# Transposing the gated product of tiles 2 to 14 by 32x32 squares on VectorE and a copy through DRAM instead of on TensorE

## The chip, the cores and the metric

The kernel runs on one core of a Trainium2 chip. The metric is the device time of one execution in microseconds. Engines are named as in the profile: PE (TensorE, with PEld for its weight loads), DVE (VectorE), ACT (ScalarE), POOL (GpSimd), SP (SyncE, whose queue issues nearly all transfers).

## What is computed

Three steps in a row, on 2304 tokens (4 sequences of 576) with 512 features:

```python
scores = scale * (q @ k.T); scores = where(0 <= i - j < 64, scores, -1e9)      # 8 heads of 64
x = softmax(scores) @ v                                                        # [2304, 512]
x = ((x @ w_a) * (x @ w_b)) @ w_out                                            # d_ff = 1536
logits = x @ phi                                                               # 32 slots, 4 for each of 8 experts
slot_input = softmax(logits, over tokens).T @ x
slot_out[e] = relu(slot_input[e] @ w1[e]) @ w2[e]                              # 512 -> 1024 -> 512
out = softmax(logits, over slots) @ slot_out
```

The weights moe_w_a, moe_w_b and moe_w_out arrive as doubles and are turned into float32 on the chip.

## The kernel before

Tokens are worked on in 18 tiles of 128. The gated product g = (x @ w_a) * (x @ w_b) of a tile is [128 tokens, 1536], made in three blocks of 512 columns, each in two halves: twelve matmuls into psa, which ACT copies to SBUF, and twelve into psb, which DVE multiplies with that copy into g (line 459). (The third block's halves are 24 matmuls of half the width.) w_out is never applied to the tokens: w_out @ phi is computed once (wphi, by project_phi), so the logits are g @ wphi, and the slots gather sums of g, which pass through w_out at the end.

The logits contract over the 1536 columns of g, so g is needed with its columns on the partitions. r_t does that for one block: four PE transposes of 128x128 (by the helper at line 142) into a PSUM tile, and an ACT copy into gT. r_l then runs twelve matmuls per tile (the profile counts two passes of each, so 24), wphi as weights and gT as the moving operand, into four groups of 32 partitions (lps). r_k, r_d and r_u follow: running maxima and sums over the tokens, a softmax over the slots, and g weighted by it into the sums acc.

PE's order is written out by hand. Its unit is a slot: the events entered for that slot with `at`, then one half block of the product. A tile has six slots in the steady state. With done[t, 2] for the slot of a tile's last half block, the logits r_l stand at slot R[t], and R[t] is done[t, 2] + 3 or, where that is later, four slots after the tile before. In a slot, the attention of a tile two further on (att_s, att_n, att_pt, att_pv, att_q, att_k) stands ahead of the r_ events. The start (up to slot 24) is a list of its own, STARTUP, in which the blocks of tiles 0 and 1 are transposed. The other engines' orders, SP's queue included, are laid out by the compiler's scheduler, from readiness and the order of the program; each engine runs its own in order.

SP issues the loads of q, k and v (lda is the 128 rows of v that begin 64 rows ahead of the tile, ldb the tile's own), each into a single buffer, at slots tied to the attention that frees it. At slot lastA = 93, when the attention of the last tile is done, open_ex gives its memory and other buffers to the experts' weights, and fetch starts to load: first w_out's float32 copy (wo_dram), then w1 and w2, into slots in a fixed sequence: two "as1", two "gT1" (buffers of gT), three "e" of the pool ex1, then seven "y", "z", "g" and so on. The pool ex1 holds the raw w_out and w_b pieces during the start, and nothing between then and these loads.

Of the kernel before, what the change touches and what calls it, by code (L numbers as in the profile page):

```python
# [11 lines left out]
F32 = mybir.dt.float32  # L12
# [51 lines left out]
HUGE = 3.0e38  # L64
# high words of the doubles 2**-127 and (just under) 2**128, read as float32
DBL_LO = float(np.array([896 << 20], np.int32).view(np.float32)[0])
# [4 lines left out]
def swa_glu_softmoe_kernel(  # L71
# [50 lines left out]

# [1 line left out]
    ident = const.tile([P, P], F32, name="ident")  # L124
# [10 lines left out]
    def turn(tag):  # L135
        """The tag's two halves in turn; the first alone once the second holds what the end needs."""
        t = turns[tag]
        t[0] = (t[0] + 1) % t[1]
        return f"{tag}{t[0]}"
# [40 lines left out]

# [1 line left out]
    att_stack = ExitStack()  # L182
# [38 lines left out]
    def att_z():  # L221
        """Zeros in the place of each pair's other head."""
        nc.gpsimd.memset(qTs, 0.0)

    # the first tiles' q as it is, two tiles in turn; the others' with zeros beside each head's part
    def att_q(t):
# [80 lines left out]
    def att_n(t, b):  # L307
        """The rows' sums divide."""
        st = sts[t]
        h = slice(4 * b, 4 * b + 4)  # L310
        rs = small.tile([P, 4, 1], F32, tag="rs", name="rs")
        r2 = rs.rearrange("p u o -> p (u o)")
        nc.vector.tensor_scalar(out=r2, in0=st["sm"][:, h], scalar1=EPS, scalar2=None, op0=ALU.add)
        yield
        nc.vector.reciprocal(out=r2, in_=r2)
        yield
        pr = st["pr"][b]
        eng = nc.gpsimd if t <= NFIRST else nc.vector
        eng.tensor_tensor(out=pr, in0=pr, in1=rs.to_broadcast([P, 4, P]), op=ALU.mult)  # L319
# [35 lines left out]

# [1 line left out]
    whi, wlo = {}, {}  # L357
# [4 lines left out]
    def decode(t, st):  # L362
        """Raw doubles st [P, n, 2] to float32 t [P, n]; out of float32's range: to 0 or its largest."""
        hi, lo = st[:, :, 1], st[:, :, 0]
        i = t.bitcast(I32)
        nc.scalar.activation(out=t, in_=hi.bitcast(F32), func=ACTF.Abs)
        yield
        nc.vector.tensor_scalar(out=t, in0=t, scalar1=DBL_LO, scalar2=DBL_HI, op0=ALU.max, op1=ALU.min)  # L368
        yield
        nc.vector.tensor_scalar(  # L370
            out=i, in0=i, scalar1=3, scalar2=0x3FFFFFF8, op0=ALU.logical_shift_left, op1=ALU.bitwise_and
        )
        yield
        nc.vector.scalar_tensor_tensor(  # L374
            out=i, in0=hi, scalar=-(1 << 30), in1=i, op0=ALU.bitwise_and, op1=ALU.bitwise_or
        )
        yield
        nc.vector.scalar_tensor_tensor(  # L378
            out=t.bitcast(U32), in0=lo.bitcast(U32), scalar=29, in1=t.bitcast(U32),
            op0=ALU.logical_shift_right, op1=ALU.bitwise_or,  # L380
        )
        yield
# [5 lines left out]

    # chunk j of a block: rows 128j.., all 512 columns; of the last block rows 256c.., columns 256h.., j = 2h + c
    def stage_w(nm, fg, j):  # L390
# [43 lines left out]
    def glu(t, fg, nm, halves=None):  # L434
        """Half of a block of the product: x @ w_a, or x @ w_b and the product of both."""
        if t not in gts:
            gts[t] = gp.tile([P, DFF], F32, tag="g", name="g")
        xhi, xlo = xts[t]
        if fg < NFG - 1:
            parts = [(0, slice(0, 512))]  # L440
        else:
            parts = [(h, slice(256 * h, 256 * h + 256)) for h in (halves or range(2))]
        ps = ps_ab.tile([P, 512], F32, tag=nm, name=f"ps{nm}")
        for h, cols in parts:
            n = 0
            for kk in range(KD):
                wh, wl = w_part(whi, nm, fg, kk, h), w_part(wlo, nm, fg, kk, h)
                for l, r in ((xhi, wh), (xhi, wl), (xlo, wh)):
                    nc.tensor.matmul(ps[:, cols], lhsT=l[:, kk], rhs=r, start=(n == 0), stop=(n == 3 * KD - 1))  # L449
                    n += 1  # L450
                yield
        cols = slice(parts[0][1].start, parts[-1][1].stop)
        if nm == "a":
            asb = p2.tile([P, 512], F32, tag=turn("as"), name="asb")
            nc.scalar.copy(out=asb[:, cols], in_=ps[:, cols])  # L455
            pas[t, fg] = asb
        else:
            gcols = slice(512 * fg + cols.start, 512 * fg + cols.stop)
            nc.vector.tensor_tensor(out=gts[t][:, gcols], in0=ps[:, cols], in1=pas.pop((t, fg))[:, cols], op=ALU.mult)  # L459

# [1 line left out]
    stats = {}  # L462
    rst = {}

    def r_t(t, fg):
# [6 lines left out]
        rst[t, fg] = gT  # L472

    def bank(t, shape, nm):
        """A PSUM tile of the token tile t's routing: the last ones run beside each other."""
        if t < NTILE - 2:
            return ps_m.tile(shape, F32, tag="m", name=nm)
        return ps_s.tile(shape, F32, tag=f"s{t % 2}", name=nm)

    def r_l(t, fgs=range(NFG)):  # L480
        lps = bank(t, [P, P], "lps")
        for n, fg in enumerate(fgs):
            gT = rst.pop((t, fg))
            for i in range(4):
                nc.tensor.matmul(  # L485
                    lps[32 * i:32 * i + 32], lhsT=wphi[:, 4 * fg + i], rhs=gT[:, i],
                    start=(n == 0), stop=(n == len(fgs) - 1),
                )
# [8 lines left out]
    def r_k(t):  # L497
        """Running maxima and sums of the slots over the tokens."""
        l4 = rst[t, "l4"]
# [32 lines left out]
    def r_c(t, lk=None):  # L532
        """Softmax of a token over the slots."""
        l4 = rst.pop((t, "l4"))
# [39 lines left out]
    def project_phi(c):  # L574
        """Rows 128c.. of w_out: to float32, kept in DRAM, and times phi."""
        st = stage(ex1, "e", moe_w_out[P * c:P * c + P, :])
# [23 lines left out]

# [1 line left out]
    cts = {}  # L602
    c4s = {}

    def both(t0, tag):
        """Both parts of the tokens' softmaxes, twice."""
        n = min(4, NTILE - NLAST - t0) if t0 < NTILE - NLAST else NLAST
# [11 lines left out]
    def turn_c(t0, bank):  # L619
        """The slots to the partitions."""  # L620
        c, n = c4s.pop(t0)
        cp = bank[0].tile([P, 4, P], F32, tag=bank[1], name="cp")
        for i in range(n):
            transpose(cp[:, i], c[:, i].bitcast(F32).rearrange("p a s -> p (a s)"))
        cps[t0] = (cp, n)
# [9 lines left out]

# [1 line left out]
    exw = {}  # L637
    pool_bufs = {**wbufs, "y": N_EX2, "z": N_EX3}
    slot_halves = {"g": 3, "as1": 1, "gT1": 1, "z": 1}
    # halves of 2 KB in the order of their use  # L640
    order = [("o", c) for c in range(DFF // P)]
# [12 lines left out]
    def source(key):  # L654
        """Rows of an expert's weights that a half of a slot takes, and those that may follow in one transfer."""
        if key[0] == "o":
# [9 lines left out]
    def fetch(n=0):  # L666
        """Fills the next n slots, or all whose contents have been used."""
        while nxt[0] < len(order):
# [40 lines left out]

# [1 line left out]
    units = [(0, 0), (1, 0), (0, 1), (1, 1), (2, 0), (2, 1), (3, 0), (3, 1)] + [(t, 2) for t in range(NFIRST)]  # L711
# [17 lines left out]
    for t in range(NTILE - 1, NFIRST - 1, -1):  # L729
        sA[t] = min(first[t] - 6, sA.get(t + 1, NSLOT) - 3)  # L730
    R = {}
    for t in range(NTILE - NLAST):
        R[t] = max(done[t, NFG - 1] + 3, R[t - 1] + 4 if t else 24)
    for t in range(NFIRST, NTILE):
# [15 lines left out]
    for t in range(NTILE):  # L750
        if t < NTILE - NLAST:
            r = R[t]
            at(max(done[t, 0] + 2, r - 5), r_t, t, 0)
            at(max(done[t, 1] + 2, r - 3), r_t, t, 1)
            at(max(done[t, 2] + 1, r - 2), r_t, t, 2)
            at(r, r_l, t)
# [8 lines left out]
    for n, f, t, *x in (  # L765
# [5 lines left out]
        at(NSLOT + n, f, t, *x)  # L771
    lastA = sA[NTILE - 1] + 5
    lastfg = {fg: done[NTILE - 1, fg] + 1 for fg in range(NFG)}
# [23 lines left out]
    def run(f, *a):  # L797
        """All of a work's pieces, each for one engine."""
        pieces = f(*a)
# [33 lines left out]

# [1 line left out]
    _, sden = stats[NTILE - 1]  # L835
# [94 lines left out]
    def slots_pick(n, c):  # L930
        """Of each expert's rows those of its own slots."""
        if c == 0:
# [82 lines left out]
```

## Time and profile before

| | |
|---|---|
| median of 3 runs | 579.15 us (578.6 to 579.62) |
| span of the profiled execution | 577.4 us |
| PE busy | 540.5 us, 94% |
| DVE busy | 297.6 us, 52% |
| ACT busy | 229.8 us, 40% |
| moved by DMA | 83.00 MB |

The profile is of one execution. Its span runs from the first instruction of the program to the last; its own whole time isn't listed, so the median of the runs stands beside the span, 1.75 us above it. Times inside the profile are counted from the start of the span. In the chain of waits each piece is the work that the next one waited for, or the one before it on the same engine.

### The profile page before, as it was taken

The numbers are of one execution on the slowest core, as the hardware profiler recorded it, in microseconds if no ns is written. First come the engines' busy times: TensorE is split into PE (matmuls) and PEld (weight loads), VectorE is DVE, ScalarE is ACT, GpSimd is POOL, SyncE is SP. The second block draws the span as 40 slices with busy tenths as digits, with TensorE's granted clock in tenths as the row PEclk, the third lists the DMA queues.
The fourth block names the chain that finished last, engine by engine and source line by source line (L and its number), as shares of the span: only waits on it lengthen the run. The fifth ranks groups of instructions, "written<-read, shape, count | busy, mean of one in ns | idle before, by whom it ended". The sixth has DMA issues, their size and how long they took to land.

```text
span 577.4 us, 11537 instructions
## 1 busy us (share of the span) xinstructions
PE 540.5 (94%) x4531; PEld 429.9 (74%) x4531; DVE 297.6 (52%) x861; ACT 229.8 (40%) x675; POOL 76.5 (13%) x110
## 2 busy tenths in 40 slices
PE   4588899999999999999999999999999999989993
PEld 3476667889887879787888888888888767953442
DVE  3999999974444444353634443454555311142222
ACT  5767664544524343443523333433454211133013
POOL 4555465331000000000000000000000000020000
PEclk9789899999999999999999999999999999999997
DMA  9975747495030302020212203022212499889997
GB/s 267 266 224 182 242 137 212 145 257 183 0 75 1 75 18 58 18 57 19 56 27 48 56 19 74 17 59 56 56 38 74 152 351 339 317 289 346 341 357 245
DMA packets 110822, 83.00 MB, mean 144 GB/s; under 512 B 77616, under 2 KB 98608, under 8 KB 110768
## 3 DMA queue, kind: packets, MB, share of 16 engines
q1 hardware_dynamic: 109808, 79.12, 46.2%
q0 software_dynamic: 960, 3.15, 1.4%
q8 instruction: 36, 0.59, 0.4%
q14 instruction: 18, 0.15, 0.1%
HBM read 74.38 MB, written 7.86 MB: 142 GB/s over the span
## 4 chain that ended last, share of the span: by engine, by line
PE 77%; DVE 13%; DMA 4%; issue 2%; ACT 1%; SPq 1%; POOL 0%; POOLq 0%; ACTq 0%
PE psb L449 24%; PE psa L449 23%; PE tg L142 5%; PE s L283 4%; PE xps L342 3%; PE lps L485 3%; PE tp L142 2%; PE ups L560 2%; PE h L883 2%; DVE w L374 2%; DVE w L378 2%; PE ops L917 2%; DMA st<-in_moe_w_a_dram 2%; DVE w L368 1%; PE tq L142 1%
## 5 line engine op out<-in xcount | busy, mean ns | idle before, releaser
L449 PE MATMUL psa<-wha,x 128*128 128x512 f32 (+1 forms) x576 | 160.4, 347 | 2.1 <-DVE x L352 1.2
L449 PE MATMUL psb<-whb,x 128*128 128x512 f32 (+1 forms) x576 | 161.3, 348 | 1.1 <-DVE g L459 1.1
L449 PEld LDWEIGHTS psa<-wha,x 128*128 128x128 f32 x576 | 101.4, 189 | 18.3 <-DVE x L352 2.0
L449 PEld LDWEIGHTS psb<-whb,x 128*128 128x128 f32 x576 | 101.3, 190 | 14.7 <-issue 2.4
L449 PE MATMUL psa<-wla,x 128*128 128x512 f32 (+1 forms) x288 | 97.3, 338 | 1.2 <-POOL wla L424 1.2
L449 PE MATMUL psb<-wlb,x 128*128 128x512 f32 (+1 forms) x288 | 97.2, 337 | 0.0
L459 DVE TENSOR_TENSOR g<-psb,asb 128x512 f32<-128x512 f32 (+1 forms) x57 | 37.7, 661 | 89.2 <-PE psb L449 75.0
L455 ACT COPY asb<-psa 128x512 f32<-128x512 f32 (+1 forms) x57 | 32.1, 563 | 103.8 <-PE psa L449 103.4
L301 ACT ACTIVATE pr<-pr,nmx 128x128 f32<-128x128 f32 x144 | 55.9, 391 | 36.7 <-DVE nmx L294 36.7
L449 PEld LDWEIGHTS psa<-wla,x 128*128 128x128 f32 x288 | 54.7, 190 | 6.9 <-POOL wla L424 2.1
L449 PEld LDWEIGHTS psb<-wlb,x 128*128 128x128 f32 x288 | 54.8, 190 | 4.6 <-POOL wlb L424 0.2
L471 ACT COPY gT<-tg 128x512 f32<-128x512 f32 x54 | 31.4, 584 | 37.1 <-PE tg L142 37.0
L252 POOL COPY kTs<-kTs 128x256 f32<-128x256 f32 x17 | 8.2, 480 | 270.8 <-DVE kTs L263 266.1
L142 PE MATMUL tg<-ident,g 128*128 128x128 f32 x216 | 33.9, 280 | 0.7 <-DVE g L459 0.4
L331 DVE COPY pT<-tp 128x512 f32<-128x512 f32 x13 | 9.0, 691 | 47.9 <-PE tp L142 47.9
L294 DVE CUSTOM_DVE_ANT_0 pr<-s,masks 128x128 f32<-128x128 f32 x144 | 32.6, 285 | 1.8 <-PE s L283 1.0
L142 PEld LDWEIGHTS tg<-ident,g 128*128 128x128 f32 x216 | 24.7, 146 | 10.5 <-issue 7.3
L301 ACT ACTIVATION_READ_ACCUMULATOR pr<-pr,nmx 128x1 f32 x144 | 27.2, 189 | 0.0
L329 ACT COPY pT<-tp 128x512 f32<-128x512 f32 x23 | 13.4, 583 | 29.7 <-PE tp L142 29.7
L142 PE MATMUL tp<-ident,pr 128*128 128x128 f32 x144 | 22.9, 282 | 1.1 <-POOL pr L319 1.1
L283 PE MATMUL s<-kTs,qTs 128*128 128x128 f32 x192 | 23.5, 275 | 0.0
L350 ACT CAST x<-xps 128x512 fp32r<-128x512 f32 x18 | 10.5, 584 | 30.8 <-PE xps L342 30.8
(138 smaller groups left out, 754.3 us busy)
## 6 DMA issues: line engine op xcount, KB each, us to landing
xw<-in_moe_w_dram SPq DMA_DIRECT2D x39, 512.0 KB, 6.8
xw<-in_moe_w_dram SPq DMA_DIRECT2D x50, 256.0 KB, 5.9
st<-in_moe_w_b_dram SPq DMA_DIRECT2D x12, 512.0 KB, 5.3
st<-in_moe_w_a_dram SPq DMA_DIRECT2D x12, 512.0 KB, 5.9
st<-in_moe_w_out_dram SPq DMA_DIRECT2D x12, 512.0 KB, 4.7
out_dram<-ob SPq DMA_DIRECT2D x18, 256.0 KB, 3.9
ldq<-in_q_dram SPq DMA_DIRECT2D x16, 256.0 KB, 3.6
ldk<-in_k_dram SPq DMA_DIRECT2D x16, 256.0 KB, 3.4
```

Of the source, the lines that this page charges most:

```text
L142: nc.tensor.transpose(o, i, ident)
L283: nc.tensor.matmul(sp[:, u], lhsT=qT[:, 2 * u + b].rearrange("p h w -> p (h w)"), rhs=kTs[:, t % 2, u, W * b:W * b + P],)
L294: nc.vector.tensor_tensor_reduce(out=pr[:, u], in0=sps[b][:, u], in1=mk, scale=1.0, scalar=HUGE, op0=ALU.add, op1=ALU.min, accum_out=nmx[: ...
L301: nc.scalar.activation(out=pr[:, u], in_=pr[:, u], func=ACTF.Exp, scale=-1.0, bias=nmx[:, i:i + 1], accum_out=sm[:, i:i + 1],)
L329: nc.scalar.copy(out=pT, in_=tp)
L342: nc.tensor.matmul(xps[W * h:W * h + W, u, W * b:W * b + W], lhsT=vt[:, 2 * u + h, :], rhs=st["pT", b][:, u, W * h:W * h + W],)
L374: nc.vector.scalar_tensor_tensor(out=i, in0=hi, scalar=-(1 << 30), in1=i, op0=ALU.bitwise_and, op1=ALU.bitwise_or)
L449: nc.tensor.matmul(ps[:, cols], lhsT=l[:, kk], rhs=r, start=(n == 0), stop=(n == 3 * KD - 1))
L455: nc.scalar.copy(out=asb[:, cols], in_=ps[:, cols])
L459: nc.vector.tensor_tensor(out=gts[t][:, gcols], in0=ps[:, cols], in1=pas.pop((t, fg))[:, cols], op=ALU.mult)
L471: nc.scalar.copy(out=gT, in_=tp)
L485: nc.tensor.matmul(lps[32 * i:32 * i + 32], lhsT=wphi[:, 4 * fg + i], rhs=gT[:, i], start=(n == 0), stop=(n == len(fgs) - 1),)
```

## The change

For tiles 2 to 14 r_b takes the place of r_t. One DVE instruction transposes the block's 64 squares of 32x32, each within its group of 32 partitions, and writes them grouped by the partition group for which they are meant (gq, in a slot "e" of ex1). Four DMAs of 64 KB, one for each group of 32 source partitions, write gq to a DRAM tile gd in runs of 512 bytes, so arranged that one more DMA of 256 KB reads it back with the columns of g on the partitions (gT, rows of 2 KB). In gT the tokens of a block of 128 columns then stand in four runs of 32 with a step of 128; r_l reads them with that step. These tiles' R is done[t, 2] + 4 in place of + 3, and R of tiles 2 to 7 stays at four slots after the tile before (32 to 52), that of 8 to 14 goes from 56, 62, ... 92 to 57, 63, ... 93. r_b of the three blocks stands at R - 6, R - 4 and R - 3. The tiles 0, 1 and 15 to 17 keep r_t.

```diff
+    def r_b(t, fg):
+        gq = ex1.tile([P, 512], F32, tag="e", name="gq")
+        nc.vector.transpose(
+            out=gq.rearrange("p (j c t) -> p c j t", j=4, c=4),
+            in_=gts[t][:, 512 * fg:512 * fg + 512].rearrange("p (c j f) -> p c j f", c=4, j=4),
+        )
+        gd = dram.tile([4, 32, 4, P], F32, tag="gd", name="gd", bufs=4)
+        for i in range(4):
+            nc.sync.dma_start(
+                out=gd[:, :, i].rearrange("j f e -> f j e"),
+                in_=gq[32 * i:32 * i + 32].rearrange("p (j e) -> p j e", j=4),
+            )
+        gT = p2.tile([P, 512], F32, tag=turn("gT"), name="gT")
+        nc.sync.dma_start(out=gT, in_=gd.rearrange("j f i e -> (j f) (i e)"))
+        rst[t, fg] = gT.rearrange("p (i c t) -> p c i t", i=4, c=4)
...
                 nc.tensor.matmul(
-                    lps[32 * i:32 * i + 32], lhsT=wphi[:, 4 * fg + i], rhs=gT[:, i],
+                    lps[32 * i:32 * i + 32].rearrange("p (i t) -> p i t", t=32) if t in by_squares else lps[32 * i:32 * i + 32],
+                    lhsT=wphi[:, 4 * fg + i], rhs=gT[:, i],
                     start=(n == 0), stop=(n == len(fgs) - 1),
                 )
...
+    lastA = sA[NTILE - 1] + 5
+    by_squares = [t for t in range(2, NTILE - NLAST) if done[t, NFG - 1] + 2 < lastA]
     R = {}
     for t in range(NTILE - NLAST):
-        R[t] = max(done[t, NFG - 1] + 3, R[t - 1] + 4 if t else 24)
+        R[t] = max(done[t, NFG - 1] + (4 if t in by_squares else 3), R[t - 1] + 4 if t else 24)
...
-            at(max(done[t, 0] + 2, r - 5), r_t, t, 0)
-            at(max(done[t, 1] + 2, r - 3), r_t, t, 1)
-            at(max(done[t, 2] + 1, r - 2), r_t, t, 2)
+            if t in by_squares:
+                for fg in range(NFG):
+                    at(max(done[t, fg] + 1, r - (6, 4, 3)[fg]), r_b, t, fg)
+            else:
+                at(max(done[t, 0] + 2, r - 5), r_t, t, 0)
+                at(max(done[t, 1] + 2, r - 3), r_t, t, 1)
+                at(max(done[t, 2] + 1, r - 2), r_t, t, 2)
```

## Rows read from the trace of the kernel before

**Rows 1.** The page: the span, and each engine's busy time, share and instructions.

```profile
span 577.4 us, 11537 instructions
...
PE 540.5 (94%) x4531; PEld 429.9 (74%) x4531; DVE 297.6 (52%) x861; ACT 229.8 (40%) x675; POOL 76.5 (13%) x110
```

**Rows 2.** Window: us, then PE, PEld, DVE, ACT, POOL busy, clock, DMA share, GB/s.

```profile
...
250.00:300.00 50.00, 50.00 (x419) 41.42 (x419) 22.28 (x83) 18.98 (x64) 0.80 (x2) 1.00 0.16 37
```

**Rows 3.** Chain of waits, one tile: start us, us, what.

```profile
...
280.06 2.87 PE psb L449 x24
...
284.82 0.44 PE tg L142 x4
...
292.18 0.79 PE lps L485 x24
...
295.93 0.62 PE xps L342 x16
296.55 0.58 PE tp L142 x4
...
297.50 0.47 PE tg L142 x4
...
306.13 0.59 PE tg L142 x4
...
317.73 0.79 PE lps L485 x24
```

**Rows 4.** Timeline of PE: start us, us, instruction.

```profile
...
265.04 0.60 PE L142 MATMUL tg<-ident,g 128*128 128x128 f32 x4
265.40 0.48 PE L449 MATMUL psa<-wha,x 128*128 128x512 f32 x1
```

**Rows 5.** Timeline of DVE behind the end of a block.

```profile
...
282.97 0.69 DVE L459 TENSOR_TENSOR g<-psb,asb 128x512 f32<-128x512 f32 x1 [0.57 <-PE psb L449]
...
285.60 0.29 DVE L552 COPY dt<-dps 128x128 f32<-128x128 f32 x1
...
286.29 0.69 DVE L319 TENSOR_TENSOR pr<-pr,rs 128x512 f32<-128x512 f32 x1
```

**Rows 6.** Timeline of SP's queue.

```profile
...
274.38 0.37 SPq L207 DMA_DIRECT2D ldb<-in_v_dram  x1
274.95 0.42 SPq L207 DMA_DIRECT2D ldq<-in_q_dram  x1
...
296.59 0.37 SPq L207 DMA_DIRECT2D lda<-in_v_dram  x1
```

**Rows 7.** Landing times of the stores, and issues of the whole run.

```profile
...
DMA to landing us min/median/max: 2.2/3.9/5.6
...
xw<-wo_dram SPq DMA_DIRECT2D x4, 256.0 KB, 2.8
```

**Rows 8.** DMA issues from 274 to 275.3 us: KB, us to landing.

```profile
...
ldb<-in_v_dram SPq DMA_DIRECT2D x1, 256.0 KB, 3.1
...
ldq<-in_q_dram SPq DMA_DIRECT2D x1, 256.0 KB, 4.6
```

**Rows 9.** DMA issues from 132 to 138 us.

```profile
...
xw<-wo_dram SPq DMA_DIRECT2D x3, 512.0 KB, 5.8
```

**Rows 10.** Waits of SP's queue from 440 to 456 us: us, times, longest.

```profile
...
SPq L695 <- PE lps L485: 12.5, 1, 12.5
```

**Rows 11.** Windows in the stretch of the experts' weights.

```profile
...
450.00:455.00 5.00, 5.00 (x58) 3.86 (x56) 2.00 (x4) 0.58 (x1) 0.00 (x0) 1.00 0.00 0
495.00:500.00 5.00, 5.00 (x44) 5.00 (x43) 0.85 (x2) 0.37 (x1) 0.00 (x0) 1.00 0.50 179
505.00:510.00 5.00, 5.00 (x55) 4.33 (x51) 2.08 (x8) 1.50 (x5) 0.00 (x0) 1.00 0.53 193
520.00:525.00 5.00, 4.84 (x49) 2.66 (x42) 2.68 (x15) 2.87 (x10) 0.00 (x0) 1.00 1.10 349
```

**Rows 12.** Chain of waits near the end.

```profile
...
555.28 5.72 DMA xw<-in_moe_w_dram
```

More of the change, by code (lines that the diff above doesn't have):

```diff
@@ L771, in swa_glu_softmoe_kernel @@
         at(NSLOT + n, f, t, *x)
-    lastA = sA[NTILE - 1] + 5
     lastfg = {fg: done[NTILE - 1, fg] + 1 for fg in range(NFG)}
```

## The prediction

> **What bounds the kernel now.** I read the page first, then the middle of the run by stretches, then the chain of waits of one tile, then DVE, SP and the DMA of the same tile, and at last the stretch in which the experts' weights stream in. The page shows one engine that hardly rests: PE is busy for 94% of the span, DVE for 52% [rows 1]. In 50 us of the middle PE has no idle time at all, at a granted clock of 1.00 (the level of 2.4 GHz), while DVE is busy for 22.28 of the 50 us and the DMA engines for 16% [rows 2]. The chain of waits of a tile is a seamless row of PE pieces [rows 3]: nothing there waits for DVE, ACT or a transfer. So in this stage a PE instruction that goes is worth what it takes, and work put on DVE and DMA is free as long as its result is there when PE's fixed order comes to it. The last 120 us are different: from about 455 us the weights stream, at 349 GB/s with the DMA engines full [rows 11], and the chain of waits passes once through a weight transfer before the last products [rows 12]. There a gain on PE counts only if the transfers start earlier too.
>
> **What goes.** Thirteen tiles (2 to 14) times three blocks: 39 groups of four PE transposes, with their 39 ACT copies out of PSUM. ACT is not on the chain, so its copies count as nothing. For a group on PE there are two readings. By the starts, a group holds up the next matmul by 265.40 - 265.04 = 0.36 us [rows 4]. By the chain, the three groups of one tile take 0.44, 0.47 and 0.59 us, mean 0.50 [rows 3]. The chain's pieces run from end to end, and the end of a matmul is modelled: part of the group's share is the tail of the instruction ahead of it. What adds up over a tile is the distance of starts. I take 0.40, nearer to the starts: 39 x 0.40 = 15.6 us. The bounds are 39 x 0.36 = 14.0 and 39 x 0.50 = 19.5.
>
> **What comes, on DVE.** One transpose of 128x512 per block. The trace has none. Nearest row: an operation of the same size from SBUF to SBUF, 0.69 us [rows 5]. Below, it can't take less than a 128x128 copy, 0.29 [rows 5]; above, I let every set of squares cost a pass of its own, 4 x 0.69 = 2.76. I take 0.69 since the elements per partition are the same. Three per tile are 2.1 us (at most 8.3) in a period of 317.73 - 292.18 = 25.55 us (logits to logits [rows 3]) in which DVE is idle for more than half [rows 2]: the cover is that idle time, and its price as load is nothing. As delay it counts in the hop below.
>
> **What comes, on SP and DMA: the hop.** A block is written in four transfers of 64 KB, SP then waits for their landing, and reads 256 KB back. Blocks 0 and 1 are transposed six and four slots of the order ahead of the logits matmuls; the tight one is block 2, with three. There the transpose is one slot after the product's last matmul, and the logits are four slots after it (three before, since the change moves the whole chain of a tile by one slot). That lead binds for tiles 8 to 14, seven tiles; the earlier ones follow each other every four slots and have more. Its length [rows 3]: the last matmul of the block ends at 282.93; the logits stood at 292.18. Moved by a slot, they come behind psa (to 295.93), the xps matmuls (0.62) and the tp transposes (0.58), but their own 0.79 and the tg group of 0.44 that stood in the stretch are gone: 295.93 + 0.62 + 0.58 - 0.79 - 0.44 = 295.90, a lead of 12.97 us.
>
> What the hop needs, from the same 282.93. The product on DVE ends at 283.66 and the transpose at 284.35: 1.42 us [rows 5]. If DVE does the next tile's eight mask operations first, and the copy dt behind them (to 285.89), it is 3.65 [rows 5]. SP needs 0.37 us an issue [rows 6], so the fourth write goes out 1.11 later. A write to DRAM lands 2.2 to 5.6 us after its issue, median 3.9 for 256 KB [rows 7]; for 64 KB I still take 3.9. Reading 256 KB of another DRAM copy took 2.8 [rows 7]; with another load just ahead 4.6 [rows 8]. Low: 1.42 + 1.11 + 2.2 + 2.8 = 7.5. Taken: 1.42 + 1.11 + 3.9 + 2.8 = 9.2. High: 3.65 + 1.11 + 5.6 + 4.6 = 15.0. The taken value is hidden with 3.7 us to spare, so the hop costs nothing. At the high end it is late by 2.0 us in seven tiles, 13.9 us. Late next would be the logits, with everything behind them on PE.
>
> Behind SP's wait for the landing stand the loads of q, k and v. Each is issued as soon as its single buffer is free [rows 6] and is wanted four slots, some 17 us, later: a wait of 4 us on SP is covered by that, and would cost its excess if it weren't.
>
> **What is rearranged.** The logits matmuls read columns in runs of 32 with a step. No row shows such a read. The bounds are nothing and as long again, 0.79 x 13 = 10.3 us. I take nothing: number and size of the matmuls stay.
>
> The transpose's buffer takes the three slots "e". Before, three weight loads of 512 KB went into them at 132 to 138 us, far ahead of their use [rows 9]. Now these 1.57 MB come at the end: at 349 GB/s [rows 11] that is 4.5 us of transfer. Besides, SP's stream waits for the last regular tile's logits (12.5 us before the change [rows 10]), which come one slot, 3.0 us, later against PE's order. Upper bound 7.5 us of delay. Against it: from 450 to 455 the DMA engines are empty, and in 495 to 500 and 505 to 510, where the stream waits for PE to release buffers, they idle for 2.5 and 2.4 us [rows 11]. The early loads [rows 9] went out as soon as their buffers were free, so I expect the moved ones in the empty stretch, and the 3.0 us in the 4.9 us of idle time: nothing. With nothing used of the empty stretch it is 7.5 - 4.9 = 2.7 us.
>
> **Sum.** 577.4 - 15.6 = 561.8 us of span. The median of the runs shown is 579.15, or 1.75 above the span of the profiled execution; that stays: 563.6 us.
>
> **The rivals.**
> 1. *The hop is partly late.* For: its high end. Against: four terms must all be high at once. From 563.6 (just late) to 577.5 (2.0 us in seven tiles); halfway 570.6.
> 2. *SP's order makes it slower.* SP issues in order, and lda waits for PE's xps matmuls: it went out at 296.59 [rows 6], or 295.36 with the 1.23 us that have gone. If the order puts the writes behind it, they start at 295.7, and 1.11 + 3.9 + 2.8 later it is 303.5: 7.6 us late in seven tiles, 53 us, or 617. It decides from a delay of (15.6 + 1.2) / 7 = 2.4 us a tile, a hop of 15.4 us. Against: the writes are ready ten microseconds before lda is, and the order of before follows readiness [rows 9].
> 3. *The four writes go one after the other.* If each takes its whole landing time, 4 x 3.9, the hop is 1.42 + 15.6 + 2.8 = 19.8, late by 6.9 in seven tiles: 611.6. Two transfers issued 0.57 us apart speak against it: ldb landed at 277.48 and ldq, of equal size, at 279.55 [rows 6, 8], 2.07 us later and not another 3.1 or more. A quarter of the bytes would add about 0.5 for each write, 5.5 in all for the landing, inside the bounds above. The Trainium skill, "DMA: Bandwidth & Descriptors", section "Rules for kernel authors", holds that transfers to disjoint groups of partitions share the same engines and serialize, and that one transfer over all partitions should be made of them; this change does the contrary. The rows of ldb and ldq bear it out for the bytes alone.
> 4. *The reordered read slows the logits*: 10.3 us, 573.9.
> 5. *The tail keeps something*: 2.7 us, 566.3.
>
> **How the numbers follow.** A change of 0.2%, 1.2 us, is about what a measurement of this kernel tells from none. Chances: the forecast, with its own range 559.7 (19.5 us saved) to 565.2 (14.0), 0.60; rival 1 0.15; rival 5 0.07; rival 4 0.06; rivals 2 and 3 0.09 together; and 0.03 that losses just cancel. Faster is 0.60 + 0.15 + 0.07 + 0.06 less 0.02 for the top of rival 1: 0.86. Same 0.05, slower 0.09. The range goes from 559.5 to 573.5, so that rivals 2, 3 and the upper end of 1 and 4 are left out. The prediction is 563.6 us.
>
> **What the profile after would show.** PE still without idle time in the middle, and a tile's period (25.55 us) shorter by 1.2. On DVE 39 new instructions of about 0.7 us. On SP five more issues per block, the read some 4 us behind the first write. If rival 1, 2 or 3 holds, PE idles ahead of the logits matmuls, released by the read of gT; if rival 4, a group of 24 logits matmuls takes over 0.79; if rival 5, the wait of PE for weights near the end grows beyond 5.72 us [rows 12]. The prediction is wrong above all if DVE or SP takes the new work in another order than it becomes ready.

## The result and the profile after

The changed kernel takes 563.97 us (median of 4 runs, 562.8 to 564.65) against 579.21 us before (4 runs): 0.9737 of the time, 95% interval 0.9723 to 0.9751. That is 15.2 us less; the forecast was 563.6 us.

The page of the changed kernel: the span, and busy time, share and instructions of each engine.

```profile
span 562.2 us, 11580 instructions
...
PE 523.5 (93%) x4375; PEld 412.0 (73%) x4375; DVE 318.7 (57%) x900; ACT 208.6 (37%) x636; POOL 77.3 (14%) x110
...
L477 DVE STREAM_TRANSPOSE gq<-g 128x512 f32<-128x512 f32 x39 | 27.6, 709 | 1.0
...
gd<-gq SPq DMA_DIRECT2D x156, 64.0 KB, 1.8
gT<-gd SPq DMA_DIRECT2D x39, 256.0 KB, 3.3
```

156 matmuls are gone from PE (39 groups of four) and 17.0 us of its busy time [rows 1]; 39 transposes of 709 ns have come to DVE, 195 issues to SP. The same window of the middle as before [rows 2], in the same columns:

```profile
250.00:300.00 50.00, 50.00 (x423) 41.72 (x422) 27.69 (x93) 16.38 (x59) 0.81 (x2) 1.00 0.42 108
```

PE still has no idle time there, at a granted clock of 1.00. DVE went from 22.28 to 27.69 us, the DMA engines from 16% to 42% of the time: room that was there.

The chain of waits of a tile (start us, us, what), to be laid beside rows 3:

```profile
273.13 2.95 PE psb L449 x24
276.09 1.78 PE s L283 x16
...
288.85 0.79 PE lps L502 x24
...
313.18 0.79 PE lps L502 x24
...
337.50 1.00 PE lps L502 x24
362.00 0.79 PE lps L502 x24
```

A tile's period is 313.18 - 288.85 = 24.33 us in place of 25.55 [rows 3]: 1.22 less for three groups, 0.41 each. The lead from the last matmul of block 2 (276.09) to the logits is 12.76 us. A group of logits matmuls takes 0.79 as before [rows 3], so the read with a step costs nothing. One group has 1.00; more of it below.

The hop of that tile, from the timelines of DVE and SP:

```profile
276.12 0.69 DVE L459 TENSOR_TENSOR g<-psb,asb 128x512 f32<-128x512 f32 x1 [0.23 <-PE psb L449]
276.85 0.71 DVE L477 STREAM_TRANSPOSE gq<-g 128x512 f32<-128x512 f32 x1
...
279.15 0.29 DVE L570 COPY dt<-dps 128x128 f32<-128x128 f32 x1
```

```profile
277.59 1.80 SPq L483 DMA_DIRECT2D gd<-gq  x4
281.20 0.34 SPq L488 DMA_DIRECT2D gT<-gd  x1
```

DVE takes the transpose right behind the product, ahead of the next tile's mask operations and the copy dt. The four issues end at 279.39, the read goes out at 281.20 and lands 2.6 us later (the only read issued from 277 to 285 us), at 283.8: 7.7 us after the last matmul, 5.1 ahead of need.

### The profile page after: what moved, and what is told of

Same layout as the page of the kernel before. It is cut to its first block, busy times and chain, and to the rows that moved or that the text cites. A ratio compares the mean times of both kernels' runs of the same rounds, so it can differ in the third digit from the quotient of the medians.

```text
span 562.2 us, 11580 instructions
## 1 busy us (share of the span) xinstructions
PE 523.5 (93%) x4375; PEld 412.0 (73%) x4375; DVE 318.7 (57%) x900; ACT 208.6 (37%) x636; POOL 77.3 (14%) x110
## 4 chain that ended last, share of the span: by engine, by line
PE 70%; DVE 13%; DMA 11%; issue 2%; ACT 2%; SPq 1%; POOL 1%; ACTq 0%
PE psb L449 24%; PE psa L449 23%; DMA xw<-in_moe_w_dram 7%; PE s L283 3%; PE xps L342 3%; PE lps L502 3%; PE tp L142 2%; PE ups L578 2%; DVE w L374 2%; DMA st<-in_moe_w_b_dram 2%; DVE w L378 1%; DMA wo_dram<-wo 1%; DVE w L370 1%; PE tg L142 1%; PE s L279 1%
## 5 line engine op out<-in xcount | busy, mean ns | idle before, releaser
L477 DVE STREAM_TRANSPOSE gq<-g 128x512 f32<-128x512 f32 x39 | 27.6, 709 | 1.0
L283 PEld LDWEIGHTS s<-kTs,qTs 128*128 128x128 f32 x192 | 22.4, 192 | 0.1
L368 DVE TENSOR_SCALAR w<-w 128x512 f32<-128x512 f32 x24 | 16.0, 666 | 8.5 <-ACT w L366 8.5
```

Of the source, the lines that this page charges most:

```text
L283: nc.tensor.matmul(sp[:, u], lhsT=qT[:, 2 * u + b].rearrange("p h w -> p (h w)"), rhs=kTs[:, t % 2, u, W * b:W * b + P],)
L477: nc.vector.transpose(out=gq.rearrange("p (j c t) -> p c j t", j=4, c=4), in_=gts[t][:, 512 * fg:512 * fg + 512].rearrange("p (c j f) -> p ...
```

## The experiments

All ratios are to the kernel before, run on the same chip beside each kernel. Edits are shown against the changed kernel, shortened where they have "...".

**The gain without the hop.** r_b is reduced to one copy:

```diff
-        gq = ex1.tile(...); nc.vector.transpose(...); gd = dram.tile(...); 4 x nc.sync.dma_start(out=gd..., in_=gq...)
-        nc.sync.dma_start(out=gT, in_=gd...)
+        nc.scalar.copy(out=gT, in_=gts[t][:, 512 * fg:512 * fg + 512])
```

> r_b is cut down to one ACT copy of the untransposed block into gT: no PE transpose, no DVE transpose, no transfer. The transposition is left out, so the logits are of other data. Theory (the gain is the PE time of 39 groups, and the hop through DVE, SP and DRAM is hidden): as the changed kernel, 563 to 565 us, ratio to the kernel before 0.972 to 0.976. Rival (the hop takes back part of a larger gain): below 562. Rival (ACT's relief from its 39 copies is part of the gain): above 566, since 39 copies of the same size are back on ACT.

563.58 us, 0.9732 (0.9716 to 0.9748): the changed kernel's time. With nothing in place of the PE transposes but a copy on ACT there is no more to gain, so the hop costs less than these runs tell apart. And the 39 ACT copies, back in this kernel, aren't part of the gain.

**The hop without the gain.** The events and gT of before, with r_b's work added and its read sent to a spare buffer "e" (this edit is shown against the kernel before):

```diff
+                    at(max(done[t, fg] + 1, r - (6, 4, 3)[fg]), r_b, t, fg)
             at(max(done[t, 0] + 2, r - 5), r_t, t, 0)
...
+        gT = ex1.tile([P, 512], F32, tag="e", name="gq")
         nc.sync.dma_start(out=gT, in_=gd.rearrange("j f i e -> (j f) (i e)"))
```

> The PE transposes and ACT copies of before feed the logits, and beside them DVE transpose, four writes and read of each block are all done, the read going to a buffer that nobody uses; the order is shifted by one slot as in the changed kernel. Theory (the added work is free): 578.5 to 580 us, ratio 0.999 to 1.002. Rival (DVE, SP or DMA load costs something that the changed kernel pays out of a larger gain): 581 or more.

579.36 us, 0.9998 (0.9988 to 1.0008). The same load on DVE, SP and DMA, with the order shifted by a slot, costs nothing where PE keeps its transposes. These two runs close the account: as closely as their intervals tell, all of the 15 us are PE's.

**How long the hop may be.** The lead is shortened:

```diff
-        R[t] = max(done[t, NFG - 1] + (4 if t in by_squares else 3), R[t - 1] + 4 if t else 24)
+        R[t] = max(done[t, NFG - 1] + 3, R[t - 1] + 4 if t else 24)
```

and with `2 if t in by_squares else 3` in the other run.

> As the changed kernel, but the logits stay three slots behind the last block's product instead of four: the lead is about 4 us shorter, some 8.5 to 9 us, against a hop of about 8.4 by the trace. Theory (hop of 8.4): 563 to 566 us, PE waiting for the read by 0 to 0.4 us in some of seven tiles. Rival (hop of 9.2, as predicted): 565 to 568. Rival (the hop is 11 or more): above 578.

> As the changed kernel, but the logits two slots behind the last block's product: a lead of about 4.6 us for tiles 9 to 14, less than the hop. Theory (hop of 8.4): late by 3.8 us in six tiles, 563.97 + 23 = 587 us. Rival (hop of 9.2): 591. Rival (the waits are made good elsewhere, since PE is not the bound): 570 or less.

Two slots: 581.54 us, 1.0035 (1.0017 to 1.0054), slower than before. Three: 569.01, 0.9822 (0.9806 to 0.9839). The chain of waits with two slots shows the hop by itself, and the list of PE's waits (us, times, longest) what it cost in all:

```profile
325.49 2.89 PE psb L449 x24
...
328.47 0.70 DVE g L459
...
329.19 0.71 DVE gq L477
...
331.26 1.78 DMA gd<-gq
...
333.18 2.54 DMA gT<-gd
...
335.76 0.42 PE lps L502 x8
```

```profile
PE lps L502 <- DMA gT<-gd: 13.7, 6, 3.8
```

From 328.37 (end of psb) to 335.76 it is 7.4 us. PE waited for reads 13.7 us in six tiles: less than the 23 expected, because the logits of blocks 0 and 1 go ahead and cover part, and the hop is a microsecond shorter than the 8.4 that I had put in.

With three slots PE waited 3.96 us in one tile and 0.33 in another, nowhere else. In the first, SP's queue shows why:

```profile
327.67 7.58 SPq L483 DMA_DIRECT2D gd<-gq  x5
335.43 0.34 SPq L488 DMA_DIRECT2D gT<-gd  x1
335.82 1.41 SPq L483 DMA_DIRECT2D gd<-gq  x3
```

Five writes stand together: block 2's four and the first of the next tile's block 0, which waits for a product not yet made (DVE's transpose of it began at 334.20). The read that PE needs stands behind it. The changed kernel has the same order in the same tile:

```profile
326.46 8.54 SPq L483 DMA_DIRECT2D gd<-gq  x5
335.18 0.34 SPq L488 DMA_DIRECT2D gT<-gd  x1
```

There the read is 0.2 us late: it is the group of 1.00 above. The fourth slot, which leaves 3.0 to 6.4 us between the landing of the last read and the logits in the other six tiles where the lead binds (8, 9 and 11 to 14), is used up in this one.

Behind a long wait PE's granted clock fell. In the run with three slots, two windows, one in the wait and one behind it, in the columns of [rows 2]:

```profile
334.00:338.00 4.00, 0.38 (x16) 0.11 (x4) 0.88 (x2) 0.43 (x1) 0.00 (x0) 1.00 0.44 101
340.00:342.00 2.00, 2.00 (x6) 1.60 (x5) 0.00 (x0) 0.00 (x0) 0.00 (x0) 0.50 0.46 131
```

The clock, 1.00 before, is 0.50 (the level of 1.2 GHz) from 340 to 342 and 1.00 again from 344. With two slots it stood at 0.50 from 390 to 392 and from 452 to 456, behind waits of 2.23 and 3.84 us. That run is 17.6 us behind the changed kernel, 3.9 more than it waited; windows of 2 us (0.50 and 0.80, then 0.50, 0.50 and 0.59) put what the clock cost PE there at 4.2 us, an estimate. In the changed kernel the clock is 1.00 all the way from 130 to 500 us.

**The order on SP's queue.** Three runs at three slots tried to take the read from behind that write. First, reads on ACT's queue:

```diff
-        nc.sync.dma_start(out=gT, in_=gd.rearrange("j f i e -> (j f) (i e)"))
+        nc.scalar.dma_start(out=gT, in_=gd.rearrange("j f i e -> (j f) (i e)"))
```

> The lead of three slots again, but the read of gT is issued from ACT's queue; the four writes stay on SP's. In the run with three slots, PE waited 4.0 us for a read that stood on SP behind the first write of the next tile's block, which waited for DVE. Theory (SP's order makes the hop long; the hop by itself is 7.4 us): 563.5 to 565.5 us, no such wait of 4 us. Rival (the hop is 11 to 12 us by itself): 568 to 570 again. Rival (ACT's queue now waits for the writes to land, 1.8 us three times a tile, and holds up the softmax): 566 to 572, PE waiting for ACT.

569.57 us, 0.9834 (0.9809 to 0.9859). PE waited for reads 4.9 us in three tiles, 2.3 at most: in one of them the read went out at 334.11, behind an ACT copy of pT that waits for PE itself. The queue behind a late instruction had only moved.

Then one DRAM buffer:

```diff
-        gd = dram.tile([4, 32, 4, P], F32, tag="gd", name="gd", bufs=4)
+        gd = dram.tile([4, 32, 4, P], F32, tag="gd", name="gd", bufs=1)
```

> The lead of three slots once more, with one DRAM buffer for gd instead of four: a block's writes then have to wait for the read of the block before, so no write can stand ahead of that read on SP. Reads stay on SP. Theory (the hop by itself is 7.4 to 8.4 us, and what made it 12 was a read queued behind the next tile's first write): 563.5 to 566 us, no wait of PE above 1 us ahead of the logits. Rival (a lead of 8.5 us is too short even in good order): 567 or more, with PE waiting 0.5 us or more for gT in most of the tiles 8 to 14.

568.37 us, 0.9811 (0.9794 to 0.9828), and the same wait of 4.0 us. SP's compiled order was that of the first run with three slots, instruction for instruction: the edit changed nothing, and the run is a repetition.

Last, SP in the order of the program:

```diff
-    with tc.manual_schedule(engines=MANUAL):
+    with tc.manual_schedule(engines=MANUAL | {mybir.EngineType.SP}):
         for n in range(SPLIT, STOP or NSLOT + 8):
```

> The lead of three slots, and SP's queue in the order of the program during the slots, as PE's is: each block's read stands right behind its own four writes. (The one buffer for gd, tried before, had left SP's compiled order as it was.) Theory (the wait of 4.0 us comes from a read queued behind the next tile's first write): 563.5 to 566 us, no wait of PE for gT above 1 us. Rival (a lead of 8.5 us is too short in any order): 567 or more, with waits for gT in most of tiles 8 to 14.

568.24 us, 0.9808 (0.9784 to 0.9831). The wait of 4 us is gone; PE waits for gT 0.7 us in each of two tiles. So that wait was SP's order, and three slots come within 1 us of enough in every tile. But the time isn't won. The xs matmuls of the tail (w_out applied to the slots' sums) begin 2.3 us later than in the changed kernel (506.58 and 504.32), and from there to the last weights it takes 2.2 us more. Its SP queue:

```profile
435.22 1.79 SPq L483 DMA_DIRECT2D gd<-gq  x4
438.41 0.34 SPq L488 DMA_DIRECT2D gT<-gd  x1
438.86 14.93 SPq L713 DMA_DIRECT2D xw<-wo_dram  x8
453.84 21.00 SPq L713 DMA_DIRECT2D xw<-in_moe_w_dram  x19
```

In the order of the program the loads into "e" stand behind one into "as1", for which SP waited 10.4 us until a product on DVE had released the buffer; the stream of w1 begins at 453.84 against 443.40 in the changed kernel. That is rival 5, at 2.2 us where its bound was 2.7; 1.6 of them are waits of PE for weights.

**One write and four reads.**

```diff
-        gd = dram.tile([4, 32, 4, P], ...)
+        gd = dram.tile([P, 4, P], ...)
-        for i in range(4):
-            nc.sync.dma_start(out=gd[:, :, i]..., in_=gq[32 * i:32 * i + 32]...)
-        nc.sync.dma_start(out=gT, in_=gd...)
+        nc.sync.dma_start(out=gd.rearrange("q j e -> q (j e)"), in_=gq)
+        for j in range(4):
+            nc.sync.dma_start(out=gT[32 * j:32 * j + 32]..., in_=gd[:, j].rearrange("(i f) e -> f i e", i=4))
```

> Four slots of lead as in the changed kernel, but the block is written by one transfer of 128 partitions in rows of 2 KB and read by four transfers of 32 partitions in runs of 512 bytes, in place of four writes and one read. Theory (the hop is hidden either way): 563 to 565 us. Rival (four transfers to parts of the partitions go one after the other, as the rule cited in the prediction has it): the fourth of the four reads lands four times as late after its issue as the first; by the changed kernel's trace (1.8 us median for every write) it doesn't.

563.97 us, 0.9726 (0.9706 to 0.9746). The write of 256 KB lands 2.5 us after its issue, the reads of 64 KB 2.1 (medians), though four are issued within 1.8 us: they overlap, and the split costs issues, not landings.

**The same on the attention weights.** A PE transpose group feeds xps twice per tile; for b = 1, the second 64 rows, it went the same way (att_pv then reads pT with a step):

```diff
+    def att_pb(t, b):
+        pT = att.tile([P, 512], F32, tag="pT", name="pT")
+        squares(pT, sts[t]["pr"][b], "pq")        # as r_b: DVE transpose, four writes, one read
+        sts[t]["pT", b] = pT.rearrange("p (i c t) -> p c i t", i=4, c=4)
...
-        at(s + 3, att_pt, t, 1)
+        at(s + 1, att_pb, t, 1)
```

> The changed kernel, and the transposition of the attention weights of the second 64 rows (b = 1) of tiles 5 to 14 goes the same way, by squares and DRAM, right behind the division. 10 groups more leave PE. Theory (0.41 us a group as measured, hop hidden in a lead of about 12 us): 563.97 - 4.1 = 559.9 us. Rival (SP, with 20 issues a tile and the waits for landing, gets too late): 564 or more, PE waiting for reads ahead of xps or lps.

> As the run with b = 1, and the first 64 rows (b = 0) too: 20 groups more than the changed kernel leave PE, 25 issues a tile on SP. The lead of b = 0 is some 9 us less 1 us of the shorter tile. Theory (hidden): 563.97 - 8.1 = 555.8 us. Rival (SP's order or load makes the hops late): 560 or more, with PE waiting for the reads; if each of ten tiles is 2 us late, 576.

569.52 us (0.9832, 0.9808 to 0.9856) and 571.3 us (0.9857, 0.9824 to 0.9890): both slower than the changed kernel. With both halves PE waits 12.9 us for pT's reads and the writes ahead of them, on an SP queue with 25 issues a tile. With one half PE waits for no read of pT or gT, but 11.2 us in nine tiles for the ACT copy of the half that stayed. ACT's timeline there:

```profile
263.38 0.58 ACT L479 COPY asb<-psa 128x512 f32<-128x512 f32 x1 [3.80 <-PE psa L473]
263.86 0.59 ACT L331 COPY pT<-tp 128x512 f32<-128x512 f32 x1
```

The transposes tp had been on PE at 259.82; their copy stood behind asb, which needs the following half block. The two halves' copies shared a ring of two buffers. With a buffer of its own for the new one, and then for tiles 5 to 17 in place of 5 to 14:

```diff
-        pT = att.tile([P, 512], F32, tag="pT", name="pT")
+        pT = att.tile([P, 512], F32, tag="pT1", name="pT", bufs=1)
...
-    att_squares = [(t, b) for t in range(NFIRST + 1, NTILE - NLAST) for b in (1,)]
+    att_squares = [(t, b) for t in range(NFIRST + 1, NTILE) for b in (1,)]
```

> The run that moves the attention weights of b = 1 of tiles 5 to 14 off PE too, with a buffer of its own for their transposed copy. In the run without it PE waited 11.2 us in nine tiles for the ACT copy of b = 0, which stood on ACT behind the copy of the next half block. Theory (that order came from the two copies sharing a ring of two buffers): the wait goes, 559 to 561 us. Rival (the scheduler sets ACT's order from something else): 567 to 570 again, with the same wait.

> The run with the attention weights of b = 1 off PE and a buffer of their own, now for tiles 5 to 17 in place of 5 to 14: 3 groups more. Theory (0.41 to 0.56 us a group, hidden): 558.33 less 1.2 to 1.7, 556.6 to 557.1 us. Rival (tiles 15 to 17 follow each other every three slots, and the three slots e are released later to the experts' weights): 558 or more, with PE waiting for pT or a later start of the weights' stream.

558.33 us (0.9629, 0.9605 to 0.9653) and 556.21 us (0.9600, 0.9584 to 0.9616). ACT's wait is gone, and the last kernel is 7.8 us faster than the changed one. That the ring set ACT's order is what the edit showed; how the scheduler came to it stays open.

## Why the prediction was right

**PE's share.** Forecast 0.40 us a group, 15.6 in all; the period gives 0.41, 15.9 in all. PE's short waits from 130 to 470 us grew from 1.5 to 2.1 us, which leaves 15.3; the run without the hop has 2.1 too, so they aren't the hop's. That run confirms the term by itself: 15.6 us (579.17 - 563.58). The 0.40 was a choice between the two readings, and that it came within 0.01 is in part luck: the prediction read one start. The starts around the three groups of a tile of the kernel before, each with the next matmul of the product:

```profile
270.31 0.66 PE L142 MATMUL tg<-ident,g 128*128 128x128 f32 x4
270.72 0.48 PE L449 MATMUL psb<-whb,x 128*128 128x512 f32 x1
...
279.43 0.64 PE L142 MATMUL tg<-ident,g 128*128 128x128 f32 x4
279.82 0.36 PE L449 MATMUL psb<-whb,x 128*128 128x256 f32 x1
...
284.66 0.60 PE L142 MATMUL tg<-ident,g 128*128 128x128 f32 x4
285.02 0.47 PE L449 MATMUL psa<-wha,x 128*128 128x512 f32 x1
```

The distances are 0.41, 0.39 and 0.36, 1.16 a tile where the period lost 1.22. The starts, not the chain's pieces (0.50), were the right reading.

**DVE.** 0.71 us for a transpose, forecast 0.69. As load it is free (window above, and the run with the hop added).

**The hop.** Forecast 9.2 us against a lead of 12.97; measured 7.7 against 12.76. The term that was too large is the landing of a write: 3.9, taken from stores of 256 KB at the end of the run, against a median of 1.8. The size is the smaller part of that: in the run with one write, 256 KB landed in 2.5 in the middle of the run. Why the stores at the end took longer no run tells. A write's issue was dearer than taken, 0.43 us (median) for 0.37. The conclusion stood, but with less safety than these numbers say: the sum follows one block through idle queues, and in one tile SP's order made the hop 4 us longer. The mechanism of rival 2 was real; only what stood ahead was another (a write of the next tile, not lda), and its 4 us stayed within the fourth slot.

**Reads with a step** cost nothing: 0.79 us.

**The tail.** The loads into "e" went out where they were expected: the changed kernel's SP queue, in the stretch where before the DMA engines were empty [rows 11].

```profile
427.98 0.44 SPq L713 DMA_DIRECT2D xw<-wo_dram  x1
...
433.74 0.46 SPq L713 DMA_DIRECT2D xw<-wo_dram  x1
435.11 0.34 SPq L488 DMA_DIRECT2D gT<-gd  x1
435.50 7.86 SPq L713 DMA_DIRECT2D xw<-wo_dram  x5
443.40 0.91 SPq L713 DMA_DIRECT2D xw<-in_moe_w_dram  x2
```

And the chain near the end, to be laid beside rows 12:

```profile
504.32 2.71 PE xs L876 x24
...
508.25 7.31 DMA xw<-in_moe_w_dram
...
515.62 5.96 DMA xw<-in_moe_w_dram
...
540.56 5.79 DMA xw<-in_moe_w_dram
546.39 1.91 PE ops L940 x26
```

From xs to the last ops (the experts' second product) it is 42.07 us, before 42.25: nothing was kept. The kernel before, from its chain of waits, from SP's queue and from PE's waits:

```profile
518.79 2.71 PE xs L853 x24
...
561.04 1.92 PE ops L917 x26
```

```profile
455.10 0.38 SPq L695 DMA_DIRECT2D xw<-in_moe_w_dram  x1
```

```profile
PE ops L917 <- DMA xw<-in_moe_w_dram: 0.3, 1, 0.3
```

The 5.72 us of rows 12, by which the prediction would have known rival 5, is the time of a transfer (now 5.79) and no wait of PE: PE waited 0.3 us for weights there before, and the changed kernel's list of waits has none. The later start was real: w1's stream begins 60.9 us ahead of xs (443.40 to 504.32) in place of 63.7 (455.10 to 518.79), 2.8 later against PE's order where 3.0 were forecast, and was covered. But the chain now runs through six weight transfers one behind the other, from 508.25 to 546.35, where before it passed through one: PE and the stream end together. In the run with SP in the order of the program the stream began another 8.2 us later against xs (453.84 to 506.58), and 2.2 us of that were no longer covered.

**Four writes.** Rival 3 had the four landings one after the other, 7.2 us at 1.8 each. From the first issue to the read it is 3.61 us (277.59 to 281.20), and the issues take 1.80 of them: the landings overlap. The Trainium skill, "DMA: Bandwidth & Descriptors", section "Rules for kernel authors", says that transfers to disjoint halves of the partitions serialize; for the landings of 64 KB each this trace doesn't bear it out, and for larger sizes no run here tells. Whether the bytes of the four share the engines isn't shown: the DMA engines were busy for 0.30 of those 3.61 us.

## What to carry to other kernels

Where one engine has no idle time and its order is fixed, price a removed group by the distance of starts it held up, and anything added elsewhere by whether it arrives before its consumer's turn; two kernels, one with only the removal and one with only the addition, settle it. Give a chain over DMA more lead than its sum: its steps are short, but each stands in a queue, and one instruction that isn't ready, put ahead by the scheduler, adds microseconds (here 4 us of waiting, and 5 of time in all). When such a run comes out slower, look for the instruction ahead in the queue before dropping the idea: a buffer of its own turned 569.5 us into 558.3.

## What was not expected

- The round trip through DRAM is quick: a write of 64 KB landed in 1.8 us (median; 1.6 to 4.1), the read of 256 KB in 3.3 (2.5 to 5.1), and the whole hop with DVE and SP took 7.4 us where it stood by itself.
- A transposition group of the attention is worth more than one of the product: with b = 1 moved, a tile's period is 23.70 us in place of 24.33, 0.63 for one group against 0.41. The starts in the changed kernel would have told it:

```profile
312.52 0.66 PE L142 MATMUL tp<-ident,pr 128*128 128x128 f32 x4
313.11 0.86 PE L502 MATMUL lps<-gT,wphi 128*32 128x128 f32 x24
```

The group held up the logits matmuls by 0.59 us, where a group of the product held up the next matmul by 0.36 to 0.41. Why it takes longer between the xps and the logits matmuls no run tells.
